# Attention and expert layer on one core: weights and x converted earlier, inside the attention units

## The chip, the cores and the metric

One core of one Trainium2 chip. The metric is the device time of one execution in microseconds. The time before is the median of three runs.

## The reference, cut to what matters

The kernel computes a multi-head attention with a position bias made by a small network, and feeds its result to an expert layer with a clipped quadratic activation. Shapes: batch 4, heads 8, sequence 576, head size 64; tokens 2304, model 512, hidden 2048; all float32.

```python
scores = scale * q @ k.T + bias            # bias from log distances, per head
attn = exp(scores - max) / (sum + 1e-9)
x = (attn @ v).transpose(0, 2, 1, 3).reshape(B * S, H * D)
h = x @ w_in
g = where(h >= 1, h, where(h <= -1, 0, (h + 1) ** 2 / 4))
out = g @ w_out
```

## The kernel before, in words

There are three stages. The first makes the bias in HBM. The second (lines 393 to 656) is attention: 16 units n, one for each pair of heads p = n // 4 and batch b = n % 4. A unit has five parts k of 128 query rows; each part is cut into two half-steps, `step(2 * k)` after its scores and `step(2 * k + 1)` after the queued transposes and value products have been drained. The text counts half-steps through as T = 10 n + i. TensorE makes scores (lines 431, 432, 452, 453), transposes of the exponentials (line 497) and value products (line 535); VectorE adds the bias and takes the maximum (line 434); ACT takes exponentials (line 441) and evicts; GpSimd subtracts to get the low halves (lines 131, 482). Every operand is kept as a high and a low part (fp32r), and three products make one.

The third stage is the expert layer (lines 661 to 751). It takes three blocks of 768 tokens, in each 16 blocks f of 128 hidden columns, and for each f two halves j of 384 tokens: `up_proj` (12 matmuls of 384 columns, lines 678 to 680), the activation (lines 687 to 691), `down_proj` (9 matmuls of 512 columns, lines 699 to 701). One such (f, j) is called a half-step of the expert stage; there are 96. It needs two things in SBUF. The weights of f: `weights(f)` calls `weight` for w_in and for w_out (lines 104 to 122): a load of 128 x 512 int64 (512 KB), two ACT operations that make floats of the two words (lines 113, 114), a VectorE join (line 115), an ACT cast to the high part (line 117), a GpSimd subtraction for the low part (line 118). And x of head pair k and half j: `split_x` (line 344) loads both heads' value products and the inverse sums that attention stored in HBM (`xT`, `rT`), adds, multiplies, casts to the high part on ACT (line 383) and subtracts for the low part.

The tables `XA` and `WT` of CFG say when this is done for the first two weight blocks and the first token block. Before the change that is in units 14 and 15: each x has a pair (unit, part) at which it is asked for and one at which it is made, and the weights of f = 0 and 1 are traced at unit 15, parts 1 and 4. Six of the eight x (mode 'p') are made with GpSimd doing add, multiply and subtraction (lines 378, 379, 385), pinned there by `pool` up to unit 14; the two of mode 'v' use VectorE (lines 381, 382, 387).

The order of instructions on an engine is set by the framework's scheduler, which takes what it believes ready, in the order written; `tc.keep_in_program_order` pins an instruction behind the one written before it on its engine. SP issues almost all DMAs, in order. One buffer each of the tags `raw`, `a` and `x` in the pool `rps[0]` serves both kinds of conversion; two bias tiles also use `x` (line 404). From the third block on, the weights are converted during the expert stage, in tiles that lie in memory which the attention stage holds (lines 662 to 670).

Of the kernel before, what the change touches and what calls it, by code (L numbers as in the profile page):

```python
# [30 lines left out]
CB = sum(CBW)  # L31
CFG = dict(un=('paaa',) * NG, xa=((((14, 0), (14, 1), '', 'p'), ((14, 2), (14, 4), '', 'p'), ((14, 4), (15, 0), '', 'p'), ((14, 3), (15, 1), 'bias', 'p')), (((15, 0), (15, 1), 'kh', 'p'), ((15, 0), (15, 2), 'kl', 'v'), ((15, 1), (15, 3), 'vs', 'p'), ((15, 1), (15, 4), '', 'v'))), ex=(9, 2, 0, 2, 9), bb=5, mv=1, hi='pvvpv', rb='a', lag=(1, 1), dr=(3, 1, 2, 2, 2), pool=((0, 1), (2, 0), (2, 1), (3, 0), (3, 1)), sb=4, keep=1, drain=2, diag='a', rb2='v', eps='v', rc=2, rbb=1, hb=2, rawb=(2, 2), t=(3, 10, 11, 10, 18, 11, 12, 19), eb=4, seq=0, pb=(6, 9, 12, 14, 16), pq=22, tb=6, ub=12, low0='ppp', anch=(8, 8, 16, 23, 23), low1='ppp', ob=6, gb=3, fin=2, wt=((15, 1), (15, 4)), lastp=15, xs=2, sbf=('v', 'v', 'v', 'v', 'v'), bsE=(), ytail='p')
EPS = 1e-9
RB = 2
LASTP = CFG["lastp"]
XA = CFG["xa"]
NX = [((14, 0), (14, 1), (14, 1), (15, 0)), ((4, 0), (6, 0), (8, 0), (10, 0))]
WT = CFG["wt"]
# [8 lines left out]
def attn_cpb_moe_kernel(ctx, tc, qk, vL, cb, win, wout, lw, ident, ii, out):  # L47
# [52 lines left out]
    def x_pool():  # L100
        turn[1] += 1
        return ring[turn[1] % len(ring)]

    def weight(src, dst, name):
# [12 lines left out]
        nc.scalar.copy(h, t.bitcast(F32))  # L117
        nc.gpsimd.tensor_tensor(out=l, in0=t.bitcast(F32), in1=h.bitcast(F32), op=ALU.subtract)  # L118

    def weights(f):  # L120
        weight(win[f], [x.rearrange("p a b -> p (a b)") for x in wi[f]], f"i{f}")
        weight(wout[f * P : f * P + P], wo[f], f"o{f}")
# [4 lines left out]
    def low(o, i, h, x="p"):  # L127
        if x == "v":
            nc.vector.tensor_tensor(out=o, in0=i, in1=h.bitcast(F32), op=ALU.subtract)
            return  # L130
        pool(nc.gpsimd.tensor_tensor(out=o, in0=i, in1=h.bitcast(F32), op=ALU.subtract))

    def pool(ins):
        if KEEP and go[0]:
            tc.keep_in_program_order(ins)
# [208 lines left out]
    def split_x(blk, k, j, early=False, raw=None):  # L344

        src = xT[k][blk // TB][:, :, TH * j : TH * j + TH].rearrange("(s d) i c -> d s i c", s=2)
        if raw is None:
            rp, n_ = x_pool()
            if n_:
                r = rp.tile([P, 3, TH], F32, tag="x", name=f"x{blk}_{k}_{j}", bufs=n_)  # L350
                r, rr = r[:, 0:2], r[:, 2]
            else:
                r = rp.tile([P, 2 * DM], F32, tag="raw", name=f"x{blk}_{k}_{j}")[:, : 2 * TH].rearrange("p (a b) -> p a b", a=2)
                rr = rp.tile([P, DM], F32, tag="a", name=f"xr{blk}_{k}_{j}")[:, :TH]
        else:
            r, rr = raw[:, 0:2], raw[:, 2]
# [12 lines left out]

        z = (2 * (blk // TB) + j) % 3  # L370
        h = x_tile(z, k, 0, f"xh{blk}_{k}_{j}")
        l = x_tile(z, k, 1, f"xl{blk}_{k}_{j}")
        xs[blk, k, j] = h, l
        x = r[:, 0]

        def parts():
            if early == "p":
                pool(nc.gpsimd.tensor_tensor(out=x, in0=x, in1=r[:, 1], op=ALU.add))
                pool(nc.gpsimd.tensor_tensor(out=x, in0=x, in1=rr, op=ALU.mult))
            else:  # L380
                nc.vector.tensor_tensor(out=x, in0=x, in1=r[:, 1], op=ALU.add)  # L381
                nc.vector.tensor_tensor(out=x, in0=x, in1=rr, op=ALU.mult)
            nc.scalar.copy(h, x)
            if early == "p":
# [4 lines left out]
        if early:  # L389
            return parts  # L390
        parts()

    with ExitStack() as ph:
        tp1 = ph.enter_context(tc.tile_pool(name="a_eT1", bufs=1))
# [131 lines left out]
        def values(n, half, es, eT, vs):  # L526
            hi, lo = eT
            b, p = n % B, n // B
            w = 256 + D * half
            x = sp.tile([P, 2, 320], F32, tag="x", name=f"x{n}_{half}", bufs=2)  # L530
            for j in range(2):
                ps = psO.tile([P, 512], F32, tag="T", name=f"O{n}_{half}_{j}")
                for src, first, last in ((hi, True, False), (lo, False, True)):
                    for tb in range(4):
                        nc.tensor.matmul(ps[:, :w], vs[:, 4 * j + tb, :], src[:, 4 * j + tb, :], start=first and tb == 0, stop=False)

                    nc.tensor.matmul(ps[:, :w], vs[:, 8 + j, :], src[:, 8, :], start=False, stop=last)
                nc.scalar.copy(x[:, j, :w], ps[:, :w])
            c0 = b * S + 256 * half
            c1 = c0  # L540
            while c1 < c0 + w:
                e = min(c0 + w, c1 - c1 % TB + TB)
                dst = xT[p][c1 // TB][:, :, c1 % TB : c1 % TB + e - c1]
                stores.append([CFG["xs"], dst, x[:, :, c1 - c0 : e - c0]])
# [6 lines left out]
        xe = {}  # L551

        def drain(keep, mid=None, at=0):
            while len(queue) > keep:
# [4 lines left out]
                    f()  # L559

        stores = []

        def store_x(all_=False):
            for s_ in stores:
                s_[0] -= 1
            while stores and (all_ or stores[0][0] < 0):
                _, dst, x = stores.pop(0)
                nc.sync.dma_start(out=dst, in_=x)

        def step(i_):  # L570
            store_x()
            for m in range(3):
                for t, i in STEPS:
                    if t == 20 - 10 * m + i_ and 0 < n + m < N:
                        preps[n + m][i]()

        go[0] = True
        for n in range(N):
# [6 lines left out]
            for k in range(5):  # L585
# [46 lines left out]
                    x[0] -= 1  # L632
                drain(CFG["dr"][k], exp_, CFG["ex"][k])
                exp_()
                last_e = exps[-1]
                step(2 * k + 1)
                for i in range(NK):
                    for j in range(2):
                        ask, make, home, e = XA[j][i]
                        if (n, k) == ask:  # L640
                            r = None
                            if home:
                                po, w, n_ = dict(kh=(qp, QW, CFG["hb"]), kl=(qp, QW, 2), vs=(qp, 10 * P, 2), bias=(bp, 2 * S, CFG["bb"]))[home]
                                r = po.tile([P, w], F32, tag=home, name=f"rx{j}_{i}", bufs=n_)
                                r = r[:, : 3 * TH].rearrange("p (a b) -> p a b", a=3)
                            xe[i, j] = split_x(0, i, j, e, r)
# [172 lines left out]
```

## Time and profile before

| | us |
|---|---|
| three runs | 770.16, 762.58, 764.74 |
| median | 764.74 |
| the profiled execution | 770.81 |
| its span | 769.0 |
| TensorE busy in the span | 717.0 |

The profile is of one execution, and its rows are times of that one. Busy time of TensorE counts instructions that overlap, so a stretch can be full and still leave small holes.

### The profile page before, as it was taken

What the parts mean: (1) busy time and instruction counts of PE and PEld (TensorE: products, weight loads), DVE (VectorE), ACT (ScalarE), POOL (GpSimd) and SP (SyncE); (2) the same over time, 40 slices, a digit from 0 to 9 for tenths busy, and PEclk for the clock granted to TensorE, in tenths of its full rate; (3) what the DMA queues carried; (4) which work ended last, traced back from release to release, by engine and by line L of the source; (5) the groups of instructions that cost most, each with busy time, mean ns of one, the idle gap of its engine ahead of it and who ended that gap; (6) DMA issues with size and microseconds to landing.
All of it is one profiled execution on the core that took longest, in us unless ns stands there. A gap on an engine that the chain in (4) does not pass through costs nothing. (4 is left out here: it accounts for less than half of the span.)

```text
span 769.0 us, 13382 instructions
## 1 busy us (share of the span) xinstructions
PE 717.0 (93%) x4688; PEld 635.8 (83%) x4688; DVE 445.7 (58%) x907; ACT 475.1 (62%) x1041; POOL 419.6 (55%) x362
## 2 busy tenths in 40 slices
PE   5677899899999999787899999999999999999997
PEld 2324899899999999775888889999998999989996
DVE  6998788778878888574665734663222243222222
ACT  7996889879989899596798562432222243222222
POOL 8985688858887888864688442222222222222221
PEclk9999999999999999898999999999999999999999
DMA  8887878956987887437665422461000011000002
GB/s 241 264 250 234 228 186 216 259 152 154 277 233 184 230 188 180 117 100 236 203 218 168 147 94 82 117 180 43 1 1 0 1 40 64 0 1 1 1 0 83
DMA packets 58515, 103.35 MB, mean 134 GB/s; under 512 B 12480, under 2 KB 32464, under 8 KB 58448
## 3 DMA queue, kind: packets, MB, share of 16 engines
q1 hardware_dynamic: 56000, 92.44, 41.7%
q0 software_dynamic: 2304, 9.96, 6.4%
q8 instruction: 37, 0.61, 0.4%
q14 instruction: 30, 0.25, 0.1%
q10 hardware_dynamic: 144, 0.09, 0.1%
HBM read 67.38 MB, written 25.12 MB: 120 GB/s over the span
## 5 line engine op out<-in xcount | busy, mean ns | idle before, releaser
L691 POOL TENSOR_TENSOR gl<-c,gh 128x384 fp32r<-128x384 f32 x96 | 100.7, 1049 | 243.1 <-ACT gh L690 222.3
L688 ACT ACTIVATE c<-c,half_s 128x384 f32<-128x384 f32 x96 | 59.0, 615 | 158.0 <-DVE c L687 157.4
L687 DVE TENSOR_SCALAR c<-h 128x384 f32<-128x384 f32 x96 | 53.2, 554 | 140.0 <-PE h L680 132.6
L482 POOL TENSOR_TENSOR lo<-c,hi 128x512 fp32r<-128x512 f32 x75 | 103.0, 1387 | 44.4 <-DVE hi L481 42.0
L678 PE MATMUL h<-xh,wi 128*128 128x384 f32 x352 | 120.1, 341 | 7.1 <-DVE c L689 4.3
L680 PE MATMUL h<-xh,wi 128*128 128x384 f32 x352 | 118.8, 338 | 0.5 <-POOL wi L118 0.5
L679 PE MATMUL h<-xl,wi 128*128 128x384 f32 x352 | 118.4, 336 | 0.3 <-DVE xl L387 0.3
L699 PE MATMUL y<-wo,gh 128*128 128x512 f32 x288 | 112.7, 393 | 2.6 <-ACT wo L117 2.6
L701 PE MATMUL y<-wo,gl 128*128 128x512 f32 x288 | 114.8, 399 | 0.0
L700 PE MATMUL y<-wo,gh 128*128 128x512 f32 x288 | 114.7, 398 | 0.0
L434 DVE CUSTOM_DVE_ANT_0 e<-S,bias 128x576 f32<-128x576 f32 x128 | 94.8, 751 | 23.6 <-PE S L432 22.2
L441 ACT ACTIVATE e<-e,mx 128x576 f32<-128x576 f32 x128 | 100.5, 787 | 11.5 <-DVE mx L434 11.3
L431 PE MATMUL S<-kh,qa 128*128 128x288 f32 x256 | 79.0, 327 | 7.8 <-DMA kh<-kh 4.2
L689 DVE TENSOR_TENSOR c<-h,c 128x384 f32<-128x384 f32 x96 | 53.3, 556 | 54.9 <-ACT c L688 54.7
L690 ACT CAST gh<-c 128x384 fp32r<-128x384 f32 x96 | 49.1, 512 | 52.6 <-DVE c L689 51.7
L678 PEld LDWEIGHTS h<-xh,wi 128*128 128x128 f32 x352 | 66.1, 188 | 15.8 <-DVE c L689 8.9
L432 PE MATMUL S<-ls,qa 128*128 128x288 f32 x256 | 74.4, 308 | 0.0
L497 PE MATMUL T<-id_s,e 128*128 128x128 f32 x512 | 69.3, 277 | 3.7 <-ACT e L441 3.7
L679 PEld LDWEIGHTS h<-xl,wi 128*128 128x128 f32 x352 | 66.1, 188 | 2.9 <-DVE xl L387 0.5
L680 PEld LDWEIGHTS h<-xh,wi 128*128 128x128 f32 x352 | 66.0, 188 | 0.9 <-POOL wi L118 0.8
L699 PEld LDWEIGHTS y<-wo,gh 128*128 128x128 f32 x288 | 54.6, 190 | 11.7 <-ACT wo L117 2.9
L701 PEld LDWEIGHTS y<-wo,gl 128*128 128x128 f32 x288 | 54.6, 190 | 11.6
(121 smaller groups left out, 1521.7 us busy)
## 6 DMA issues: line engine op xcount, KB each, us to landing
bias_d<-y SPq DMA_DIRECT2D x36, 295.5 KB, 4.6
qk<-in_qk_dram SPq DMA_DIRECT2D x16, 608.0 KB, 4.9
qa<-in_qk_dram POOLq DMA_DIRECT2D x16, 608.0 KB, 7.1
rawi<-in_win_dram SPq DMA_DIRECT2D x16, 512.0 KB, 4.1
rawo<-in_wout_dram SPq DMA_DIRECT2D x16, 512.0 KB, 3.8
x<-xT SPq DMA_DIRECT2D x40, 192.0 KB, 3.5
v<-in_vL_dram SPq DMA_DIRECT2D x16, 320.0 KB, 3.9
qa<-ls SPq DMA_DIRECT2D x32, 152.0 KB, 4.8
```

The source lines that it names most:

```text
L431: nc.tensor.matmul(ps[:, hf, :HS], qs[:, qc], kh[:, kc : kc + HS], start=True, stop=False)
L432: nc.tensor.matmul(ps[:, hf, :HS], q0[:, qc], kl[:, kc : kc + HS], start=False, stop=True)
L434: nc.vector.tensor_tensor_reduce(out=ev.rearrange("p (a b) -> p a b", a=2), in0=ps[:, :, :HS], in1=bias[k][:, S * j : S * j + S].rearrange ...
L441: lambda ev=ev, j=j: nc.scalar.activation(ev, ev, AF.Exp, bias=mx[:, j : j + 1], scale=-1.0, accum_out=sm[:, 4 * j + k : 4 * j + k + 1])
L482: r = nc.gpsimd.tensor_tensor(out=lo, in0=m, in1=hi.bitcast(F32), op=ALU.subtract)
L678: nc.tensor.matmul(ps[:, :TH], wh_, xh, start=k == 0, stop=False)
L679: nc.tensor.matmul(ps[:, :TH], wh_, xl, start=False, stop=False)
L680: nc.tensor.matmul(ps[:, :TH], wl_, xh, start=False, stop=k == NK - 1)
L691: nc.gpsimd.tensor_tensor(out=gl, in0=c, in1=gh.bitcast(F32), op=ALU.subtract)
L699: nc.tensor.matmul(y, gh[:, c], wo[f][0], start=f == 0, stop=False)
L700: nc.tensor.matmul(y, gh[:, c], wo[f][1], start=False, stop=False)
L701: nc.tensor.matmul(y, gl[:, c], wo[f][0], start=False, stop=f == NF - 1)
```

## The change

`XA` and `WT` go. Two tables of half-steps take their place: `XQ` for x (load at T, buffer, first operation at T1) and `WQ` for the weights (load at T, first operation at T1). `step` runs the jobs of its half-step. A weight piece has three: at T1 the two ACT operations, at T1 + 1 the join and the cast to the high part, both on VectorE (the cast was ACT's), at T1 + 2 GpSimd's subtraction. An x has three: add and multiply on VectorE, cast on ACT, subtraction on GpSimd, in consecutive half-steps. `keep` pins all of them except GpSimd's, which `pool` pins in units before the last; the loads are not pinned. The eight x use the buffers `raw`, `x` and one bias tile, and no longer those of k and v. Weight pieces: units 5, 6, 9 and 10. x: pairs 0, 1 and 2 of the first half in units 4, 8 and 12, the others in units 13, 14 and 15.

```diff
+XQ = {(0, 0): (39, "raw", 43), (1, 0): (79, "raw", 83), (2, 0): (118, "raw", 123), (3, 0): (137, "bias", 142),
+      (0, 1): (125, "x", 136), (1, 1): (131, "raw", 145), (2, 1): (139, "x", 151), (3, 1): (148, "raw", 155)}
+WQ = {(0, 0): (49, 53), (0, 1): (59, 63), (1, 0): (89, 93), (1, 1): (99, 103)}
...
+    def weight_ahead(f, o):
...
+        def load():
+            w["raw"] = rps[0].tile([P, DM, 2], I32, tag="raw", name=f"raw{f}{o}")
+            nc.sync.dma_start(out=w["raw"].rearrange("p a b -> p (a b)"), in_=src.bitcast(I32))
+
+        def shift():
+            raw = w["raw"]
+            w["a"] = rps[0].tile([P, DM], F32, tag="a", name=f"a{f}{o}")
+            keep(nc.scalar.activation(raw[:, :, 0], ...
+            keep(nc.scalar.activation(w["a"], ...
+
+        def join():
+            t = w["a"].bitcast(I32)
+            keep(nc.vector.scalar_tensor_tensor(out=t, in0=t, scalar=3, in1=w["raw"][:, :, 0], op0=ALU.logical_shift_left, op1=ALU.bitwise_or))
+            keep(nc.vector.tensor_copy(h, w["a"]))
+
+        def rest():
+            pool(nc.gpsimd.tensor_tensor(out=l, in0=w["a"], in1=h.bitcast(F32), op=ALU.subtract))
...
+        def scaled():
+            for op, in1 in ((ALU.add, r[:, 1]), (ALU.mult, rr)):
+                a = nc.vector.tensor_tensor(out=x, in0=x, in1=in1, op=op)
+                if home:
+                    keep(a)
+
+        def high():
...
+            a = nc.scalar.copy(xs[blk, k, j][0], x)
+            if home:
+                keep(a)
+
+        def rest():
+            h, l = xs[blk, k, j]
+            if home:
                 pool(nc.gpsimd.tensor_tensor(out=l, in0=x, in1=h.bitcast(F32), op=ALU.subtract))
...
+        for kj in XQ:
+            plan_x(*kj)
+        for fo, (T, T1) in WQ.items():
+            load, fs = weight_ahead(*fo)
+            plan(T, load)
+            for i, f in enumerate(fs):
+                plan(T1 + i, f)
...
         def step(i_):
             store_x()
+            for f in jobs.pop(10 * n + i_, ()):
+                f()
...
-                        if (n, k) == ask:
...
-                        if (n, k) == make:
-                            xe[i, j]()
-                for f in range(2):
-                    if (n, k) == WT[f]:
-                        with tc.issue_after(last_e.ins):
-                            weights(f)
```

## Rows read from the trace of the kernel before

**Rows 1.** Windows, one unit each: stretch, then length and busy us by engine, PEclk, DMA.

```profile
237.57:253.52 15.95, 15.86 (x126) 15.34 (x125) 13.41 (x34) 14.61 (x39) 13.38 (x12) 1.00 0.74 177
...
301.34:324.31 22.97, 18.98 (x126) 18.11 (x125) 15.06 (x33) 14.68 (x40) 20.00 (x19) 0.85 0.52 134
324.31:344.90 20.59, 16.85 (x127) 15.56 (x126) 14.23 (x33) 17.60 (x46) 13.38 (x14) 1.00 0.37 100
```

**Rows 2.** Timeline of unit 14 (ACT, GpSimd, VectorE): start, us, engine, line, [idle before].

```profile
310.61 0.51 ACT L383 CAST xh<-rx 128x384 fp32r<-128x384 f32 x1 [2.80 <-POOL rx L379]
...
314.71 0.51 ACT L383 CAST xh<-x 128x384 fp32r<-128x384 f32 x1 [3.11 <-POOL x L379]
...
325.56 0.51 ACT L383 CAST xh<-x 128x384 fp32r<-128x384 f32 x1 [2.05 <-POOL x L379]
...
306.71 2.92 POOL L131 TENSOR_TENSOR ls<-qk,kh 128x608 fp32r<-128x608 f32 x2
...
308.09 3.39 DVE L161 CAST vs<-v 128x640 fp32r<-128x640 f32 x1 [1.07 <-PE O L537]
```

**Rows 3.** Windows, the hand-over between the stages.

```profile
350.00:370.00 20.00, 13.91 (x55) 10.82 (x53) 9.18 (x15) 13.50 (x25) 7.21 (x6) 0.83 0.80 248
```

**Rows 4.** Waits of TensorE from 352 to 376: us in total, times, longest.

```profile
PE y L699 <- ACT wo L117: 2.6, 1, 2.6
PE h L678 <- DVE c L689: 2.0, 1, 2.0
PE h L678 <- ACT xh L383: 1.9, 1, 1.9
```

**Rows 5.** Chain that ended last, expert stage: start, us, what.

```profile
453.48 0.17 PE h L680
...
694.20 0.24 PE y L700
...
731.88 0.24 PE y L700
764.75 0.24 PE y L701
```

**Rows 6.** Timeline, end of the attention stage (TensorE, SP).

```profile
349.57 0.27 PE L521 MATMUL R<-id_s,sum 128*9 128x128 f32 x1
...
353.42 3.12 SPq L108 DMA_DIRECT2D rawi<-in_win_dram  x2
```

**Rows 7.** Timeline, single instructions of ACT, GpSimd and VectorE.

```profile
282.63 0.83 DVE L149 CAST kh<-qk 128x1216 fp32r<-128x1216 f32 x1
...
357.39 1.28 POOL L118 TENSOR_TENSOR wo<-ao,wo 128x512 fp32r<-128x512 f32 x1 [3.68 <-ACT wo L117]
...
357.85 0.77 ACT L113 ACTIVATE rawi<-rawi,floor_s 128x512 int32<-128x512 uint16 x1
358.52 0.66 ACT L114 ACTIVATE ai<-rawi 128x512 f32<-128x512 f32 x1
...
362.10 0.60 ACT L117 CAST wi<-ai 128x512 fp32r<-128x512 f32 x1
```

**Rows 8.** Instructions by source line: ns min/median/max, first to last start.

```profile
L115 DVE SCALAR_TENSOR_TENSOR ao<-ao,rawo x16: 678/693/912, 355.5 to 458.2; 128x512 int32<-128x512 int32 x16
...
L161 DVE CAST vs<-v x16: 484/1073/3394, 33.7 to 308.1; 128x640 fp32r<-128x640 f32 x16
...
L381 DVE TENSOR_TENSOR x<-x x17: 543/552/1646, 350.6 to 622.6; 128x384 f32<-128x384 f32 x17
...
L385 POOL TENSOR_TENSOR xl<-x,xh x3: 993/998/1012, 315.6 to 334.1; 128x384 fp32r<-128x384 f32 x3
...
L108 SPq DMA_DIRECT2D rawi<-in_win_dram x16: 327/328/1040, 4.5 to 408.3; - x16
```

**Rows 9.** Windows, four us within unit 4.

```profile
144.00:148.00 4.00, 3.92 (x30) 3.51 (x29) 4.00 (x11) 3.76 (x9) 2.01 (x2) 1.00 1.05 256
```

**Rows 10.** Timeline of TensorE at the end of unit 4.

```profile
152.58 0.38 PE L431 MATMUL S<-kh,qa 128*128 128x288 f32 x1 [2.13 <-DMA kh<-kh]
```

More of the change, by code (lines that the diff above doesn't have):

```diff
@@ L31 @@
 CB = sum(CBW)
-CFG = dict(un=('paaa',) * NG, xa=((((14, 0), (14, 1), '', 'p'), ((14, 2), (14, 4), '', 'p'), ((14, 4), (15, 0), '', 'p'), ((14, 3), (15, 1), 'bias', 'p')), (((15, 0), (15, 1), 'kh', 'p'), ((15, 0), (15, 2), 'kl', 'v'), ((15, 1), (15, 3), 'vs', 'p'), ((15, 1), (15, 4), '', 'v'))), ex=(9, 2, 0, 2, 9), bb=5, mv=1, hi='pvvpv', rb='a', lag=(1, 1), dr=(3, 1, 2, 2, 2), pool=((0, 1), (2, 0), (2, 1), (3, 0), (3, 1)), sb=4, keep=1, drain=2, diag='a', rb2='v', eps='v', rc=2, rbb=1, hb=2, rawb=(2, 2), t=(3, 10, 11, 10, 18, 11, 12, 19), eb=4, seq=0, pb=(6, 9, 12, 14, 16), pq=22, tb=6, ub=12, low0='ppp', anch=(8, 8, 16, 23, 23), low1='ppp', ob=6, gb=3, fin=2, wt=((15, 1), (15, 4)), lastp=15, xs=2, sbf=('v', 'v', 'v', 'v', 'v'), bsE=(), ytail='p')
+CFG = dict(un=('paaa',) * NG, ex=(9, 2, 0, 2, 9), bb=5, mv=1, hi='pvvpv', rb='a', lag=(1, 1), dr=(3, 1, 2, 2, 2), pool=((0, 1), (2, 0), (2, 1), (3, 0), (3, 1)), sb=4, keep=1, drain=2, diag='a', rb2='v', eps='v', rc=2, rbb=1, hb=2, rawb=(2, 2), t=(3, 10, 11, 10, 18, 11, 12, 19), eb=4, seq=0, pb=(6, 9, 12, 14, 16), pq=22, tb=6, ub=12, low0='ppp', anch=(8, 8, 16, 23, 23), low1='ppp', ob=6, gb=3, fin=2, lastp=15, xs=2, sbf=('v', 'v', 'v', 'v', 'v'), bsE=(), ytail='p')
 EPS = 1e-9
@@ L118, in weight @@
         nc.gpsimd.tensor_tensor(out=l, in0=t.bitcast(F32), in1=h.bitcast(F32), op=ALU.subtract)
+    def weight_ahead(f, o):
+        w = {}
+        src = wout[f * P : f * P + P] if o else win[f]
+        h, l = wo[f] if o else [x.rearrange("p a b -> p (a b)") for x in wi[f]]
+        def load():
[4 more added lines that the diff above has]
+            w["a"] = rps[0].tile([P, DM], F32, tag="a", name=f"a{f}{o}")
+            keep(nc.scalar.activation(raw[:, :, 0], raw.bitcast(U16).rearrange("p a (b c) -> p a b c", c=2)[:, :, 0, 1], AF.Identity, scale=2.0**-13, bias=floor_s))
+            keep(nc.scalar.activation(w["a"], raw[:, :, 1].bitcast(F32), AF.Prelu, scale=2.0**-112, alpha=-(2.0**32)))
+        def join():
[4 more added lines that the diff above has]
+            pool(nc.gpsimd.tensor_tensor(out=l, in0=w["a"], in1=h.bitcast(F32), op=ALU.subtract))
+        return load, (shift, join, rest)
     def weights(f):
@@ L131, in low, with keep @@
         pool(nc.gpsimd.tensor_tensor(out=o, in0=i, in1=h.bitcast(F32), op=ALU.subtract))
+    def keep(ins):
+        tc.keep_in_program_order(ins)
     def pool(ins):
@@ L342, in x_tile, with split_x @@
         return room[g][:, c0 : c0 + TH]
-    def split_x(blk, k, j, early=False, raw=None):
+    def split_x(blk, k, j, home=None):
         src = xT[k][blk // TB][:, :, TH * j : TH * j + TH].rearrange("(s d) i c -> d s i c", s=2)
-        if raw is None:
-            rp, n_ = x_pool()
-            if n_:
+        rp, n_ = x_pool() if home is None else (rps[0], home != "raw")
+        if n_:
+            if home == "bias":
+                r = bp.tile([P, 2 * S], F32, tag="bias", name=f"x{blk}_{k}_{j}").rearrange("p (a b) -> p a b", a=3)
+            else:
                 r = rp.tile([P, 3, TH], F32, tag="x", name=f"x{blk}_{k}_{j}", bufs=n_)
[L351 to L354, printed above, removed]
-        else:
-            r, rr = raw[:, 0:2], raw[:, 2]
+            r, rr = r[:, 0:2], r[:, 2]
+        else:
+            r = rp.tile([P, 2 * DM], F32, tag="raw", name=f"x{blk}_{k}_{j}")[:, : 2 * TH].rearrange("p (a b) -> p a b", a=2)
+            rr = rp.tile([P, DM], F32, tag="a", name=f"xr{blk}_{k}_{j}")[:, :TH]
         for i in range(2):
@@ L368, in split_x @@
             c1 = e
[L370 to L373, printed above, removed]
         x = r[:, 0]
[L376 to L384, printed above, removed]
+        def scaled():
[4 more added lines that the diff above has]
+        def high():
+            z = (2 * (blk // TB) + j) % 3
+            xs[blk, k, j] = [x_tile(z, k, i, f"x{'hl'[i]}{blk}_{k}_{j}") for i in range(2)]
+            a = nc.scalar.copy(xs[blk, k, j][0], x)
[4 more added lines that the diff above has]
+            if home:
                 pool(nc.gpsimd.tensor_tensor(out=l, in0=x, in1=h.bitcast(F32), op=ALU.subtract))
@@ L387, in parts @@
                 nc.vector.tensor_tensor(out=l, in0=x, in1=h.bitcast(F32), op=ALU.subtract)
-        if early:
-            return parts
-        parts()
+        if home:
+            return scaled, high, rest
+        scaled()
+        high()
+        rest()
     with ExitStack() as ph:
@@ L543, in values @@
                 dst = xT[p][c1 // TB][:, :, c1 % TB : c1 % TB + e - c1]
-                stores.append([CFG["xs"], dst, x[:, :, c1 - c0 : e - c0]])
+                stores.append([CFG["xs"], dst, x[:, :, c1 - c0 : e - c0], [(p, t) for t in range(c1, e)]])
                 c1 = e
@@ L550, in attn_cpb_moe_kernel @@
         queue, late = [], []
-        xe = {}
         def drain(keep, mid=None, at=0):
@@ L561, in attn_cpb_moe_kernel, with plan, plan_x, load @@
         stores = []
+        jobs = {}
+        made = set()
+        def plan(T, f):
+            jobs.setdefault(T, []).append(f)
+        def plan_x(k, j):
+            T, home, T1 = XQ[k, j]
+            def load():
+                assert all((k, t) in made for t in range(TH * j, TH * j + TH))
+                for i, f in enumerate(split_x(0, k, j, home)):
+                    plan(T1 + i, f)
[4 more added lines that the diff above has]
+            load, fs = weight_ahead(*fo)
+            plan(T, load)
+            for i, f in enumerate(fs):
+                plan(T1 + i, f)
         def store_x(all_=False):
@@ L566, in store_x @@
             while stores and (all_ or stores[0][0] < 0):
-                _, dst, x = stores.pop(0)
+                _, dst, x, of = stores.pop(0)
                 nc.sync.dma_start(out=dst, in_=x)
+                made.update(of)
         def step(i_):
             store_x()
+            for f in jobs.pop(10 * n + i_, ()):
+                f()
             for m in range(3):
@@ L634, in attn_cpb_moe_kernel @@
                 exp_()
-                last_e = exps[-1]
                 step(2 * k + 1)
-                for i in range(NK):
-                    for j in range(2):
-                        ask, make, home, e = XA[j][i]
-                        if (n, k) == ask:
[L641 to L646, printed above, removed]
-                        if (n, k) == make:
-                            xe[i, j]()
-                for f in range(2):
-                    if (n, k) == WT[f]:
-                        with tc.issue_after(last_e.ins):
-                            weights(f)
         queue += [x for _, x in late]
```

2 lines of the change are left out of this document (removed).

## The prediction

> **What bounds the kernel now.** I read the windows view first, one stretch per head pair and batch (a unit, cut at the reciprocal of its row sums). The reader sees [rows 1]: a quiet unit is 15.95 us long and TensorE is busy for 15.86 of them, so TensorE's own stream sets it; ACT leaves 1.34 us idle (14.61 busy), VectorE 2.54, GpSimd 2.57. Unit 14 takes 22.97 and unit 15 takes 20.59: 7.0 and 4.6 us over a quiet unit. In unit 14 GpSimd is busy for 20.00 and the granted clock is down to 0.85; in unit 15 ACT is the engine with the extra load (17.60).
>
> The timeline of unit 14 says why [rows 2]. ACT's cast of x (line 383) stands in its stream ahead of exponentials and waits for GpSimd's multiply three times: 2.80, 3.11 and 2.05 us, together 7.96, more than the whole excess. GpSimd is late because the pinned x work queues behind its 2.92 us of ls, and VectorE's cast of v takes 3.39 us beside it.
>
> Then the hand-over to the expert stage: the windows and the waits of TensorE [rows 3, 4]. From 350 to 370 us TensorE is busy for 13.91 of 20 at a granted clock of 0.83. It waits 2.6 us for the cast of the first w_out block, 2.0 for an activation, 1.9 for an x.
>
> Last the chain [rows 5]. In the expert stage nine half-steps take 731.88 - 694.20 = 37.68, so 4.187 each and 96 x 4.187 = 401.9 us in all; an up-projection matmul is 0.17. TensorE's last attention instruction stands at 349.57 [rows 6]; eleven of the stage's matmuls, 1.9 us, run before it. The last matmul ends at 764.75 + 0.24 = 764.99. So 764.99 - 349.57 = 415.4 us are spent on 400.0 us of work: 15.4 us are lost after the attention stage, 4 us of tail come on top, and the span of 769.0 lies inside 770.81 us.
>
> **The change, part by part.**
>
> *Taken out of units 14 and 15:* two weight blocks (four pieces of 128x512) and four of the eight x; GpSimd loses add and multiply of six x. One piece of weight costs ACT 0.77 + 0.66 + 0.60, VectorE 0.69 to 0.91, GpSimd 1.28; one x cost GpSimd or VectorE an add and a multiply, ACT 0.51, and a subtraction of 0.99 [rows 2, 7, 8].
>
> *Unit 14.* It now gets two x (pairs 3 and 1), each VectorE 2 x 0.55, ACT 0.51, GpSimd 0.99 [rows 2, 8]. Sums on a quiet unit [rows 1]: VectorE 13.4 + 2.2 = 15.6, GpSimd 13.4 + 2.0 = 15.4, ACT 14.6 + 1.0 = 15.6, all just under 15.95. No ACT cast stands behind GpSimd any more: the add and multiply are VectorE's and lie a half-step, 15.95 / 10 = 1.6 us, ahead. With three engines that full I don't expect the quiet time; bounds 15.95 and 22.97, taken at 17.5: gain 5.5.
>
> *Unit 15.* Two x remain; 0.77 + 0.66 + 0.60 = 2.0 us of weight conversion on ACT and two of four casts of x go. ACT falls from 17.60 to about 17.6 - 2.0 - 1.0 = 14.6 [rows 1, 2, 7]. Bounds 15.95 and 20.59; I take 16.7, near the quiet row: gain 3.9.
>
> *Hand-over.* Both blocks of weights and all eight x stand ready when TensorE ends attention, so the waits on wo and xh have nothing left to wait for, and where TensorE has no such waits the rows show a granted clock of 1.00 [rows 1], not 0.83. What is late next is the third weight block, whose tiles lie in memory that the attention stage holds to its end. Its raw load starts 353.42 - 349.57 = 3.85 us after that end [rows 6], its first conversion follows at 357.85, and 0.77 + 0.66 + 0.69 + 0.60 + 1.28 later it is ready [rows 7, 8]: 12.3 us after the end. The first four half-steps give TensorE 4 x 4.187 - 1.9 = 14.9 us of work until then. So it is covered by 2.6 us, if activations keep up. Of the 15.4 us lost I take 10 as won; bounds 4 (only the waits on wo and xh, 4.5, go) and 13.5 (the third block still costs something).
>
> *Weights in units 5, 6, 9 and 10.* Each such unit gets ACT 0.77 + 0.66 = 1.43 against 1.34 idle, VectorE 0.69 for the join and a cast that now is VectorE's (the nearest row is its cast of v, 0.48 to 3.39, median 1.07), GpSimd 1.28 [rows 1, 7, 8]. The idle time is in small pieces and each insertion delays exponentials or evictions that TensorE soon needs. Bounds 0 (work added to a unit that TensorE sets can't shorten it; the same holds for x) and 1.43 per unit; I take 0.8, over the middle because ACT becomes as full as TensorE: 3.2 in all, at most 5.7.
>
> *x in units 4, 8, 12 and 13.* Each adds 1.1 us on VectorE, 0.51 on ACT, 0.99 on GpSimd. Bounds 0 (inside 2.5 us of idle) and 1.6 (add, multiply and cast all on the path); I take 0.6: 2.4 in all, at most 6.4.
>
> *Loads.* Only the arithmetic is pinned. SP's loads are not: in the kernel before, the first w_in block, written in unit 15, was issued at 4.5 us, its first start [rows 8]. So a load goes out as soon as its buffer is free: the first weights right after the first x in unit 4, not in unit 5. There the DMA engines have a share of 1.05, and TensorE later waited 2.13 us for kh [rows 9, 10]. On SP, kh copies and the load of the next unit's qk are queued behind such a load. 512 KB more there cost between -1 (the load at 4.5 us is gone from the start) and 3 us; I take 0.5, since the copies of kh are written ahead of the load.
>
> A rule on VectorE and GpSimd speaks against the change. The row first: beside GpSimd's 2.92 us of ls, VectorE's cast of v took 3.39, where its shortest is 0.48 [rows 2, 8]. The Trainium skill, "SBUF — State Buffer", section "Who interferes with whom", says that a VectorE instruction with two SBUF inputs, or a cast in a two-port mode, and a GpSimd instruction that reads SBUF exclude each other for their whole length. All 24 VectorE instructions that the change places in the units (an add and a multiply for each of eight x, a join and a cast for each of four pieces) are of these kinds, and the trace agrees as far as that one row goes. By it they would run in turns with GpSimd, which is the second case below.
>
> *Sum:* gains 5.5 + 3.9 + 10 = 19.4; costs 3.2 + 2.4 + 0.5 = 6.1; net 13.3. The profiled execution's 770.81 becomes 757.5. It lies 6.1 us above the median of the three runs, so on 764.74 the same difference gives 751.4. One per cent of this, 7.6 us, is about what a measurement can tell from no change.
>
> **The rivals.**
>
> *VectorE and GpSimd take turns.* Then a unit lasts as long as both engines' exclusive work: GpSimd 13.4 plus VectorE's casts of kh and v, 0.83 + 1.07 = 1.9, is 15.3 today [rows 1, 7, 8]. A weight piece adds 1.28 + 0.69 + 0.6, so 17.9 (+1.9, four times 7.6); an x adds 0.99 + 1.1, so 17.4 (+1.4, four times 5.7); unit 14 with two x comes to 19.5 (gain 3.5, not 5.5). Net 3.5 + 3.9 + 10 - 7.6 - 5.7 - 0.5 = 3.6 gained: 761. For it: the 3.39 us cast. Against it: a late GpSimd delays only lo tiles that are used much later, so the sum need not reach TensorE.
>
> *The third weight block takes over the hand-over's idle time.* Activations and evictions of the last unit slow the first half-steps, the up-projection of the third block comes too early for its weights, and only 4 us are won there: 764.74 - 7.3 = 757.4. For it: 2.6 us of cover is little. Against it: TensorE has two down-projections in hand.
>
> *A pinned VectorE instruction waits for its x.* It stands at the head of an in-order engine; the score evictions, then exponentials and matmuls queue behind it. The loads of units 14 and 15 can only start when the last store of x has landed, and in units 4 and 8 they share DMA engines that are full. Unit 14 shows the price of such waits, 7.0 us. If it falls due in units 4, 8, 14 and 15, these last two win nothing and the first two lose 14: 14 + 6.1 - 10 = 10 us slower, 775. It decides as soon as a load lands more than a half-step, 1.6 us, after its make. Against it: four to seven half-steps, 6 to 11 us, lie between load and make.
>
> **How the numbers follow.** Forecast 0.68 (751.4; own range 744 to 757), turns 0.16 (761), third block 0.08 (757.4), late x 0.08 (775). Faster by over 1% means under 757.1: the forecast and half of the third-block case, 0.72. Within 1%: turns and the other half, 0.20. Slower: 0.08. The range, 742 to 762, leaves out the late x and the outer ends of the forecast (all gains at their upper bound less 1 us of costs would be 741).
>
> **What would show it.** Right: no ACT wait of over 1 us in unit 14, units 14 and 15 under 18 us, no TensorE wait on wo or xh after attention, granted clock near 1.00 there, the end of attention 3 us earlier and the loss after it about 5 us. Wrong: VectorE waiting on a DMA of x, weight units above 17.5 us, or new TensorE waits on the third block's wi.

## The result, and the profile after

| us | before | after |
|---|---|---|
| median of 20 runs each | 766.95 | 759.87 |
| lowest and highest | 762.58, 770.43 | 756.94, 764.44 |
| the profiled execution | 770.81 | 759.95 |
| its span | 769.0 | 758.2 |

The ratio is 0.9911, with a 95% interval of 0.9892 to 0.993: 7.1 us faster, where 13.3 were forecast. That is inside the range given, but only just within the 1% that stood for "no change".

The profile was read in three places that answer to the rows of before. First the hand-over. The windows view of the changed kernel (columns as in [rows 1]) gives the 20 us from just behind the end of attention, and the last two units' worth of time, cut at the reciprocals as there:

```profile
308.87:330.84 21.97, 19.30 (x146) 17.83 (x145) 19.59 (x43) 18.83 (x50) 19.95 (x17) 1.00 0.61 149
330.84:345.56 14.72, 14.05 (x97) 13.70 (x98) 11.12 (x26) 12.10 (x32) 2.47 (x3) 0.88 0.35 98
...
350.60:370.60 20.00, 18.85 (x100) 17.35 (x99) 11.87 (x19) 18.84 (x36) 15.67 (x12) 1.00 0.58 198
```

The last line answers to [rows 3]: TensorE is busy for 18.85 us instead of 13.91, at a granted clock of 1.00 instead of 0.83. The view of TensorE's waits from 352 to 376 us, whose three longest lines before are [rows 4], has one left:

```profile
PE h L721 <- DVE c L732: 1.2, 1, 1.2
```

The first two lines of the windows answer to the last two of [rows 1]: 36.69 us for the pair, where before it was 43.56.

Second, the units that received work. This is unit 5, then TensorE's waits from 140 to 308 us (us in total, times, longest), both of the changed kernel:

```profile
160.89:178.48 17.59, 16.44 (x126) 15.52 (x124) 16.01 (x35) 15.53 (x40) 14.26 (x13) 1.00 0.76 201
```

```profile
PE S L466 <- DVE mx L469: 3.5, 3, 1.6
PE S_L L487 <- DVE mx L469: 2.3, 2, 1.2
PE T L532 <- DVE lo L508: 0.8, 2, 0.4
```

A quiet unit is 15.95 us [rows 1]; this one is 17.59, and all its engines have over a microsecond idle. TensorE waits for score maxima (mx) from VectorE: 5.8 us in all, once each in units 4, 5, 8, 9 and 12, where the same view of the kernel before shows 0.5.

Third, lengths of the units, here cut where TensorE begins to transpose a unit's row sums (R; the first line of [rows 6] is the last of them). They are worked out from the timelines; "second profile" is the changed kernel, profiled again.

| us | before | after | second profile | x alone | weights alone |
|---|---|---|---|---|---|
| units 5, 6, 9, 10 (a weight piece each) | 63.94 | 69.81 | 69.36 | 63.79 | 68.84 |
| units 8, 12, 13 (x) | 48.08 | 51.91 | 52.30 | 51.33 | 55.09 |
| units 14 and 15 | 41.68 | 34.70 | 34.34 | 36.64 | 39.66 |
| last R to TensorE's end | 415.41 | 403.96 | 405.54 | 409.19 | 408.65 |

TensorE's end came 10.8 us earlier in the first pair of profiles (764.98 to 754.15). Of this 3.6 are unit 4's, 20.52 to 16.93. Before, that unit holds 2.6 us of waits for kh [rows 10] at a granted clock of 0.92. They belong to the execution: the kernel with the weights alone, below, is the kernel before up to the end of unit 4 and has 15.74 there, with no such wait. After, unit 4 holds an x, and that has a price which also differs by execution. Four kernels below that are alike up to unit 5 (x alone and the three with pure costs) have 16.71, 17.77, 19.03 and 17.79, and the longest wait of TensorE in each is one for a score maximum, 0.7 to 1.8 us. The other 7.2 of the 10.8 agree with the medians.

### The profile page after: what moved, and what is told of

It reads as the page before. It is cut to its first block, busy times and chain, and to the rows that moved or that the text cites. A ratio compares the mean times of both kernels' runs of the same rounds, so it can differ in the third digit from the quotient of the medians.

```text
span 758.2 us, 13397 instructions
## 1 busy us (share of the span) xinstructions
PE 712.8 (94%) x4688; PEld 631.5 (83%) x4688; DVE 457.0 (60%) x921; ACT 471.6 (62%) x1037; POOL 414.1 (55%) x352
## 4 chain that ended last, share of the span: by engine, by line
PE 63%; DMA 9%; DVE 6%; ACT 6%; issue 4%; POOL 3%; SPq 0%; DVEq 0%; ACTq 0%; POOLq 0%
PE y L743 7%; PE y L744 7%; PE y L742 7%; PE h L721 7%; PE h L723 7%; PE h L722 7%; PE O L570 7%; PE T L532 4%; PE S L466 3%; PE S L467 3%; DMA x<-xT 2%; DMA bias_d<-y 2%; DMA xT<-x 2%; PE O L572 2%; DMA rawo<-in_wout_dram 2%
## 5 line engine op out<-in xcount | busy, mean ns | idle before, releaser
L517 POOL TENSOR_TENSOR lo<-c,hi 128x512 fp32r<-128x512 f32 x75 | 101.2, 1365 | 33.9 <-DVE hi L516 31.4
L476 ACT ACTIVATE e<-e,mx 128x576 f32<-128x576 f32 x128 | 100.6, 790 | 11.7 <-DVE mx L469 11.5
L532 PE MATMUL T<-id_s,e 128*128 128x128 f32 x512 | 71.1, 275 | 2.0 <-DVE hi L516 1.0
L467 PE MATMUL S<-ls,qa 128*128 128x288 f32 x256 | 72.4, 301 | 0.0
L744 PEld LDWEIGHTS y<-wo,gl 128*128 128x128 f32 x288 | 54.0, 187 | 11.5
L532 PEld LDWEIGHTS T<-id_s,e 128*128 128x128 f32 x512 | 59.2, 142 | 4.6 <-DVE lo L508 1.3
```

The costliest lines, as they stand in the source:

```text
L467: nc.tensor.matmul(ps[:, hf, :HS], q0[:, qc], kl[:, kc : kc + HS], start=False, stop=True)
L476: lambda ev=ev, j=j: nc.scalar.activation(ev, ev, AF.Exp, bias=mx[:, j : j + 1], scale=-1.0, accum_out=sm[:, 4 * j + k : 4 * j + k + 1])
L517: r = nc.gpsimd.tensor_tensor(out=lo, in0=m, in1=hi.bitcast(F32), op=ALU.subtract)
L532: nc.tensor.transpose(ps[:, tb, :], e[:, c0 : c0 + P], id_s)
L744: nc.tensor.matmul(y, gl[:, c], wo[f][0], start=False, stop=f == NF - 1)
```

## The experiments

Each kernel ran beside the kernel before on one chip, where that took 768.76 to 769.60 us, so the ratios compare and the times do so only roughly.

**The two halves of the change.** Each kernel has one half and leaves the other as it was.

```diff
 x alone:
-        for fo, (T, T1) in WQ.items(): ...
+                for f in range(2):
+                    if (n, k) == ((15, 1), (15, 4))[f]: ... weights(f)
 weights alone:
-XQ = ...
+XA and the code that asks for x and makes it, as before
```

> Only x is made ahead; the two weight blocks are converted in unit 15 as before. Theory: units 5, 6, 9 and 10 fall back to 15.9 to 16.5 us (5.9 us less in all than with the weights in them), units 8, 12 and 13 keep 17.0 to 17.5, and the hand-over loses again the wait on the w_out block and what ACT does for it in unit 15, some 5 to 8 us: 759 to 763 us. Rival, that the hand-over is won by x alone: it stays short and the time is 753 to 756.

> Only the two weight blocks are converted ahead; x is made as in the kernel before. If the weights are paid for in their units (theory: each piece makes its unit about 1.4 us longer), units 5, 6, 9 and 10 last 17.1 to 18.0 us here too, unit 14 keeps its 25 us between two row-sum transposes, and only the wait on the w_out block and ACT's conversions leave the hand-over: 764 to 768 us. Rival, that the pieces cost nothing by themselves and the units are longer because of x: those four units are back at 15.9 to 16.5 us and the time is 759 to 762.

x alone: 760.31 us, ratio 0.9894 (0.9859 to 0.9929), as good as the whole change. Units 5, 6, 9 and 10 are quiet again: unit 5's window is 16.00 long,

```profile
156.80:172.80 16.00, 15.91 (x126) 15.40 (x124) 13.41 (x31) 14.59 (x38) 13.43 (x12) 1.00 0.82 210
```

So the weight pieces cost 69.81 - 63.79 = 6.0 us in those units, and return 5.2 after attention and 1.9 in units 14 and 15: about nothing on balance. Weights alone: 770.83 us, ratio 1.0033 (0.9999 to 1.0067), above what either theory had, even by the 769.24 us of the kernel before on this chip. Its unit 12 took 22.06. The timeline there (start, us, engine, what) says why:

```profile
277.30 0.53 SPq L108 DMA_DIRECT2D rawo<-in_wout_dram  x1
...
286.07 0.74 ACT L113 ACTIVATE rawo<-rawo,floor_s 128x512 int32<-128x512 uint16 x1 [4.59 <-DMA rawo<-in_wout_dram]
287.17 0.69 PE L540 MATMUL T_s<-id_s,e 128*128 128x128 f32 x2 [3.97 <-ACT x L567]
```

The next weight block, which nothing pins, was drawn forward from the expert stage into unit 12, where ACT waited 4.59 us for its load and TensorE 3.97 for ACT. In the changed kernel such a conversion first starts at 346.7. This kernel is therefore no clean measure of the weight half; with a quiet unit 12 it would lie at about 765, an estimate that takes this one profile's 6.1 us for every execution.

**The cast of the weights back on ACT.**

```diff
-            keep(nc.vector.tensor_copy(h, w["a"]))
+            keep(nc.scalar.copy(h, w["a"]))
```

> The cast of a weight piece goes back from VectorE to ACT, 0.60 us of ACT for 0.41 us of VectorE in each of units 5, 6, 9 and 10. Theory that VectorE and GpSimd in turns make these units long: ACT's 0.60 hides or nearly so, the four units change by -0.4 to +0.2 each and the time stays within 758 to 761. Rival that ACT is full and sets these units: each gets 0.6 longer, 762 to 763.

758.08 us, ratio 0.9852 (0.9799 to 0.9905). The four units sum to 66.88: 2.9 us less than in the changed kernel, more than the 1.6 that the theory allowed, with 0.60 us more on ACT in each. So ACT, the fullest engine by busy time, isn't what the pieces hurt.

**Pure costs in the quiet units.** Three kernels start from x alone and add two useless 128x512 instructions to each of units 5, 6, 9 and 10.

```diff
 two operands on VectorE:
+keep(nc.vector.tensor_tensor(out=t, in0=idb, in1=idb, op=ALU.add))
 one operand on VectorE:
+keep(nc.vector.tensor_reduce(out=scr[:, i : i + 1], in_=idb, op=ALU.max, ...))
 on ACT:
+keep(nc.scalar.copy(t, idb))
```

> Base: x made ahead, weights converted in unit 15, so that units 5, 6, 9 and 10 are quiet at 15.95 us. Added to each, in the half-step where the join of a weight piece stood: two VectorE instructions that read two SBUF operands of 128x512 and write one, about 0.6 us each when nothing is in their way. Nothing else of the weight piece is there. Theory that VectorE and GpSimd exclude each other: the two stand behind GpSimd's subtractions, show 0.6 to 1.6 us each, and the four units last 16.6 to 17.5. Rival that ACT's part or the load made the units of the weights long: they stay at 15.9 to 16.1.

> As the run with two-operand instructions, but the two VectorE instructions are reductions that read one SBUF operand of the same 512 elements. Theory that it is the second operand, and so GpSimd, that costs: they last about 0.6 us each wherever they stand, and the four units stay at 15.9 to 16.4, at most half of what the two-operand pair costs. Rival that any VectorE time in that place costs: the units are as long as with two operands.

> As the two runs before, but two ACT copies of 128x512, about 0.6 us each, take the place of the VectorE instructions: 1.2 us of ACT, near the 1.43 of a weight piece. Theory that ACT's idle 1.34 us take most of it: the four units last 15.95 to 16.4. Rival that ACT is full: 16.9 to 17.2.

One execution each (769.71, 761.91 and 766.34 us), so the unit lengths are what counts. On ACT, two copies of 0.61 us leave the four units at 15.85, 15.94, 15.95 and 15.94: nothing. The window of unit 5, and the added line by its source (ns, shortest, median, longest):

```profile
156.50:172.40 15.90, 15.81 (x126) 15.46 (x125) 13.38 (x32) 15.01 (x41) 12.65 (x11) 1.00 0.80 202
```

```profile
L621 ACT COPY probe<-id_s x8: 602/610/620, 165.0 to 246.7; 128x512 f32<-128x512 f32 x8
```

One-operand reductions on VectorE, 1.27 us a pair, make the units 16.56 to 17.12, 1.0 more on the mean: longer than the 16.4 that was expected, but under half of what two operands cost. Adds of two operands, in the same place, make three units 18.14 to 18.23, 2.2 more, and one 19.78, where the granted clock is 0.91 instead of 1.00. All lie above the expected 17.5. The timelines of the two kernels at that place (one operand first) show what differs:

```profile
159.79 1.30 POOL L517 TENSOR_TENSOR lo<-c,hi 128x512 fp32r<-128x512 f32 x1
...
159.84 1.27 DVE L621 TENSOR_REDUCE scr<-id_s 128x1 f32<-128x512 f32 x2
```

```profile
159.58 1.28 POOL L517 TENSOR_TENSOR lo<-c,hi 128x512 fp32r<-128x512 f32 x1
...
159.62 1.79 DVE L621 TENSOR_TENSOR probe<-id_s 128x512 f32<-128x512 f32 x1
...
161.94 0.67 DVE L621 TENSOR_TENSOR probe<-id_s 128x512 f32<-128x512 f32 x1
162.16 0.63 PE L532 MATMUL T<-id_s,e 128*128 128x128 f32 x4 [1.17 <-DVE lo L508]
```

Both meet a GpSimd subtraction at its start. The two reductions finish beside it, in 0.67 us each by source line. The first add takes 1.79, until 0.55 us after the subtraction's end (159.58 + 1.28 = 160.86, against 159.62 + 1.79 = 161.41); the second, with GpSimd idle, takes 0.67. All four pairs of adds show the same.

The add also writes 512 values a row where the reduction writes one, so this pair alone does not tell the second operand from the output. The trace of the adds does. VectorE's subtraction for the low half of a transpose has the add's shape and writes as much, but one of its operands, T, lies in PSUM:

```profile
L508 DVE TENSOR_TENSOR lo<-T,hi x53: 674/680/693, 76.6 to 345.3; 128x512 fp32r<-128x512 f32 x53
```

29 of the 53 start beside a GpSimd subtraction, and none is lengthened. Nor is every instruction with one operand free of GpSimd: the cast of v, from SBUF to SBUF, waits too. In the kernel before:

```profile
163.65 1.29 POOL L482 TENSOR_TENSOR lo<-c,hi 128x512 fp32r<-128x512 f32 x1
163.71 1.58 DVE L161 CAST vs<-v 128x640 fp32r<-128x640 f32 x1 [1.28 <-PE O L537]
```

Fourteen of its sixteen casts of v start beside a GpSimd subtraction and end 0.35 to 0.38 us after it, where the shortest cast takes 0.48 [rows 8].

**x on GpSimd, in the same half-steps.** Add and multiply of x go from VectorE to GpSimd.

```diff
-                a = nc.vector.tensor_tensor(out=x, in0=x, in1=in1, op=op)
+                a = (nc.gpsimd if home else nc.vector).tensor_tensor(out=x, in0=x, in1=in1, op=op)
                 if home:
-                    keep(a)
+                    pool(a)
```

> Add and multiply of the eight x go from VectorE to GpSimd, in the same half-steps. Theory that VectorE's two-input instructions pay for standing behind GpSimd's: units 8 and 12 lose their wait of TensorE for VectorE and shrink by 0.5 to 1.0 each, while unit 14, where GpSimd is fuller, gets 1 to 3 longer as ACT's cast waits for GpSimd again; 758 to 763. Rival that an x costs its unit the same wherever it is made: units 8 and 12 stay at 17.0 to 17.5 between two row-sum transposes.

764.96 us, ratio 0.9955 (0.9922 to 0.9988). Units 8 and 12 take 17.31 and 17.46, against 17.52 and 16.99: no shorter, as the rival had it, and unit 13 is 19.85. Unit 14 takes 22.79, 2.7 more than in the first profile of the changed kernel, as the theory had it. The timeline of ACT in unit 8:

```profile
215.74 0.51 ACT L411 CAST xh<-x 128x384 fp32r<-128x384 f32 x1 [1.91 <-POOL x L404]
```

This is the stall of [rows 2] again, now in the middle of attention: taking x off VectorE gives nothing where ACT then stands behind GpSimd.

**Later half-steps.** With the cast on ACT, three kernels move the weight pieces (`WQ`) and the x of units 4, 8 and 12 (`XQ`) within their units.

```diff
 both by three half-steps:   WQ first operation 53 -> 56, ...   XQ 43 -> 46, 83 -> 86, 123 -> 126
 weights by two:             WQ first operation 53 -> 55, ...   XQ as in the change
 weights by two, x by three: WQ first operation 53 -> 55, ...   XQ 43 -> 46, 83 -> 86, 123 -> 126
```

> The changed kernel with the cast of the weights on ACT, and with the weight pieces and the x of units 4, 8 and 12 made three half-steps later in their units, where GpSimd waits about 2 us for VectorE in a quiet unit. Theory of the turns: join, add and multiply show 0.55 to 0.8 us instead of 0.85 to 1.73, units 5, 6, 9 and 10 fall to 15.95 to 16.4 and units 8 and 12 to 16.0 to 16.5, so 2 to 4 us less than with the cast alone: ratio to the kernel before 0.978 to 0.984. Rival that the place within the unit makes no difference: units as with the cast alone, ratio 0.985.

> The kernel with the cast of the weights on ACT, with the weight pieces of units 5, 6, 9 and 10 begun at half-steps 55, 65, 95 and 105 (join at 56, 66, 96, 106) instead of 53, 63, 93 and 103. Theory (what a piece costs is VectorE's time, and the join runs long only when it meets a GpSimd instruction): at half-step 6 GpSimd has its idle time ahead of the low halves, so the join takes about 0.7 us instead of 0.9 to 1.4, and the four units sum to 65.5 us or less (quiet 63.8, cast on ACT 66.9); ratio to before 0.980 to 0.986. Rival (the join's length sets nothing, any inserted instruction costs about 0.7 us a unit by pushing the next score eviction back): the four units stay at 66.5 to 67.5, whatever the join takes; ratio 0.984 to 0.988.

> The kernel with the cast of the weights on ACT, weight pieces begun at half-steps 55, 65, 95 and 105, and x of units 4, 8 and 12 begun at 46, 86 and 126 instead of 43, 83 and 123. Theory (each VectorE microsecond put into a unit lengthens it by nearly as much, and its length is short where GpSimd idles): the four weight units sum to 66.0 to 66.6 (quiet 63.8), units 8 and 12 to 16.4 to 16.9 each as in the kernel with both later (17.3 and 17.4 with x at 83 and 123); the units of this kernel are then 3.5 + 1 us shorter than those of the changed kernel, ratio to the changed kernel on the same chip 0.991 to 0.997. Rival (what is won in the units is lost again after attention, where the kernel with both later took 405.7 instead of 404.0): same as the changed kernel, ratio to it 0.998 to 1.002.

> The changed kernel as it is, beside the kernel with the weight pieces at half-steps 55, 65, 95 and 105, for a comparison on one chip. Theory: 4 to 5 us slower than that kernel (its four weight units sum to 69.8 against 66.3, units 8 and 12 to 34.5 against 33.4), ratio to before 0.989 to 0.993. Rival: within 1.5 us of it. In either case the profile shows whether unit 4 (16.93 in the first profile of this kernel, 20.52 in that of the kernel before) is long in another execution too: if so, the wait for kh there belongs to the execution, not to the change.

Both by three: 755.87 us, ratio 0.9846 (0.9799 to 0.9893), above the 0.978 to 0.984 that was expected; the join now takes 1.41 us in every unit, since it meets a GpSimd subtraction each time, and the four units sum to 67.52. Weights by two: 757.54, ratio 0.9887 (0.9828 to 0.9945). There the join is short each time, as the theory wanted,

```profile
L139 DVE SCALAR_TENSOR_TENSOR a<-a,raw x4: 681/686/687, 160.7 to 246.2; 128x512 int32<-128x512 int32 x4
```

but the units sum to 66.30, not under 65.5: nearer to the rival. Weights by two and x by three: 759.08, ratio 0.9861 (0.9825 to 0.9897), with the changed kernel at 759.34 beside it on the same chip: no difference. Its join is as short (0.69), but the four units sum to 67.61, and TensorE's waits for kh are back there (4.5 us in all from 140 to 300). What was won in the units did not reach the total, as the rival had it; its time after attention was 406.09, the changed kernel's 405.54. The repeat of the changed kernel has unit 4 at 17.83, with a wait of 1.85 us for a score maximum and none over 0.3 for kh, and 69.36 for the four weight units.

**One x moved out of unit 14.**

```diff
-(1, 1): (131, "raw", 145), (2, 1): (139, "x", 151)
+(1, 1): (143, "bias", 150), (2, 1): (139, "x", 152)
```

> The kernel with the cast of the weights on ACT, with the x of pair 1, second half, made in unit 15 (half-steps 150 to 152) instead of unit 14 (145 to 147). That leaves one x in unit 14 and three in unit 15. Theory (what is left of unit 14's excess is the price of its two x pieces, about 2 us for each, among them TensorE's 1.6 us wait for a value product's operand and the lower granted clock behind it): unit 14 falls from 20.1 to 18 us or less, unit 15 rises by 1 to 2, TensorE's 1.6 us wait at the end of unit 14 is gone; total within 0.5% of the kernel with the cast on ACT (ratio to before 0.980 to 0.990). Rival (unit 14's excess is not from the x: it comes from the end of attention itself, where no further unit's loads and transposes fill TensorE's holes): unit 14 stays at 19.5 to 20.5, unit 15 gets longer by 1 to 2 us, ratio 0.987 to 0.992.

760.63 us, ratio 0.99 (0.9863 to 0.9938), unit 14 at 21.63. It tells nothing of the x pieces' price, for two reasons: by the cut used here half-steps 150 and 151 still lie in unit 14, and the loads of the moved x came late. Its timeline shows VectorE waiting, and TensorE behind it:

```profile
320.83 2.52 SPq L397 DMA_DIRECT2D xr<-rT  x4
321.57 0.56 DVE L404 TENSOR_TENSOR x<-x 128x384 f32<-128x384 f32 x1 [1.39 <-DMA x<-rT]
322.05 0.68 DVE L516 CAST hi<-T 128x512 fp32r<-128x512 f32 x1
...
322.88 1.09 PE L532 MATMUL T<-id_s,e 128*128 128x128 f32 x4 [2.11 <-DVE hi L516]
...
324.25 0.44 PE L466 MATMUL S<-kh,qa 128*128 128x288 f32 x1
```

A wait of 1.39 us at the head of VectorE became 2.11 on TensorE, and after it a score matmul takes 0.44 instead of 0.29: from 323 to 327 us the granted clock is 0.50, which is 1.2 GHz. So the rival "a pinned VectorE instruction waits for its x", which did not occur in the changed kernel's full units, has a real price when it does.

No version here is told apart from the change: those with the cast on ACT have ratios of 0.985 to 0.990, the changed kernel 0.9911 and 0.9878, and all these intervals overlap.

## Why the prediction was right or wrong

**Hand-over: right in size, and in its main reason.** The chain from the last R to the end went from 415.41 to 403.96 us, in the second profile to 405.54: 11.5 and 9.9 won, where 10 was taken. The waits on wo and xh are gone and the clock is at 1.00. What was said of the third weight block did not hold. The load at 353.42 [rows 6] that was taken for its own is, by the order in which the loads are written, that of the second block: only the first block's two loads, at 4.51 and 350.21, stand before it. In the changed kernel all w_in loads of line 109 belong to the third block or later ones. The first two go out 6 us before the end of attention at 350.19, so the tiles for the raw words did not wait for it, and the first low half of a w_in block is done at 355.95 + 1.30 = 357.25:

```profile
343.91 1.04 SPq L109 DMA_DIRECT2D rawi<-in_win_dram  x2
...
349.68 0.77 ACT L114 ACTIVATE rawi<-rawi,floor_s 128x512 int32<-128x512 uint16 x1 [1.13 <-DMA rawi<-in_win_dram]
...
355.95 1.30 POOL L119 TENSOR_TENSOR wi<-ai,wi 128x512 fp32r<-128x512 f32 x1
```

That is 7.1 us after the end, where 12.3 was reckoned, and TensorE waits for no wi. So the rival of the third block fell by a wider margin than the 2.6 us of cover, for a reason that the prediction did not have.

**Units 14 and 15: too high by a quarter.** 5.5 + 3.9 = 9.4 was taken; the pair gained 7.0 and 7.3 in the two profiles (6.9 by the cut of [rows 1]). Unit 15 went below the quiet time; unit 14 did not reach 17.5. No ACT cast waits 2 to 3 us for GpSimd there any more (one waits 1.00 for VectorE's multiply), but x's multiply runs long on VectorE. The timeline of the changed kernel:

```profile
328.49 2.83 POOL L517 TENSOR_TENSOR lo<-c,hi 128x512 fp32r<-128x512 f32 x2
...
328.54 1.65 DVE L404 TENSOR_TENSOR x<-x 128x384 f32<-128x384 f32 x1
...
331.07 1.16 PE L570 MATMUL O<-hi,vs 128*128 128x320 f32 x4 [1.59 <-DVE sum L677]
332.02 0.47 PE L572 MATMUL O<-hi,vs 128*128 128x320 f32 x1
...
335.47 0.31 PE L572 MATMUL O<-lo,vs 128*128 128x320 f32 x1
```

It takes 1.65 us beside GpSimd's subtractions, where 0.55 was counted; VectorE's low halves and the reciprocal of the sums queue behind it, TensorE waits 1.59 us, and then takes 0.47 instead of 0.31 for a matmul. The windows view shows why, a granted clock of 0.50, or 1.2 GHz:

```profile
332.00:334.00 2.00, 2.00 (x9) 2.00 (x9) 1.87 (x4) 0.87 (x3) 0.30 (x1) 0.50 0.11 17
```

That the long multiply causes the wait is read from this order, and no experiment shows it. Ten profiles have these x at these half-steps: in all of them the multiply takes 1.64 or 1.65 and the wait is 1.59 or 1.60. In two of them (two-operand adds, ACT copies) add and multiply of the unit's first x take 1.11 us together instead of 1.78 to 1.86, and their unit 14 is the shortest, 17.86 and 17.84 against 18.60 to 20.29.

**Weights in units 5, 6, 9 and 10: the step that failed.** 0.8 us each was taken, on the ground that "ACT becomes as full as TensorE", and the upper bound of 1.43 was ACT's time alone. Measured: 5.9 us for the four, 1.5 each, above that bound. ACT's time is free (1.21 us added, nothing lost); it is VectorE's that is on the path, though VectorE had 2.54 us idle. The mean over the four units:

| kernel | VectorE time added, us | unit longer than 15.95, us |
|---|---|---|
| ACT copies | 0 | -0.03 |
| weights by two half-steps, cast on ACT | 0.69 | 0.63 |
| weights by two, x by three, cast on ACT | 0.69 | 0.95 |
| the change, cast on ACT | 1.03 | 0.77 |
| one-operand reductions | 1.27 | 1.00 |
| both by three half-steps, cast on ACT | 1.41 | 0.93 |
| the change | 1.78 | 1.50 |
| two-operand adds (three units) | 2.46 | 2.22 |

In six of the seven kernels that give VectorE time the unit grows by 0.66 to 0.91 us for each microsecond of it. The seventh, 0.95 for 0.69, has the join of the row above it and a further wait: in each of the four units TensorE waits 0.37 us for a low half that GpSimd makes (us in total, times, longest):

```profile
PE O L570 <- POOL lo L517: 1.5, 4, 0.4
```

So GpSimd's part of a piece, 1.28 us, may cost something as well; no kernel adds it alone. The timeline of unit 5 in the changed kernel shows the path of VectorE's part:

```profile
162.09 0.74 DVE L469 CUSTOM_DVE_ANT_0 e<-S,bias 128x576 f32<-128x576 f32 x1
...
162.72 1.28 POOL L517 TENSOR_TENSOR lo<-c,hi 128x512 fp32r<-128x512 f32 x1
...
162.95 1.60 DVE L139 SCALAR_TENSOR_TENSOR a<-a,raw 128x512 int32<-128x512 int32 x1
...
164.47 0.74 DVE L469 CUSTOM_DVE_ANT_0 e<-S,bias 128x576 f32<-128x576 f32 x1
...
165.28 0.40 PE L487 MATMUL S_L<-kh,qa 128*128 128x288 f32 x1 [1.15 <-DVE mx L469]
```

The join meets GpSimd's subtraction and takes 1.60 us for its 0.69. The next score eviction stands behind it, and the next scores need the buffer that this eviction empties: TensorE waits 1.15, and as long in unit 9. In units 6 and 10 and in both kernels with VectorE instructions as pure costs the eviction that TensorE waits for is another, the low half that VectorE takes from a transpose (`lo`): 0.4 us in the change, 1.17 behind the two adds. VectorE's idle time in the quiet unit of [rows 1] is made of waits of its own, in the kernel before:

```profile
DVE vs L161 <- PE O L537: 1.1, 1, 1.1
DVE e L434 <- PE S L432: 0.9, 2, 0.6
DVE lo L473 <- POOL lo L482: 0.5, 1, 0.5
```

It lies where VectorE stands for TensorE and GpSimd; that time is no cover for work put in ahead of an eviction at another place.

**x in units 4, 8, 12 and 13: the same fault.** 0.6 each was taken; 3.8 and 4.2 us for the last three were measured, 1.3 to 1.4 each, and unit 4 lies 1.0 and 1.9 over a quiet unit. Moved by three half-steps, to a place where add and multiply take 0.55 us each, unit 12 is 16.45 and 16.48 in the two kernels that do so, where nine profiles with the early place have 16.99 to 17.50. Unit 8 is 16.86 and 18.35, inside the 16.79 to 18.99 of the early place, so nothing is settled there.

**The turns rival was nearest.** It gave 1.9 for a weight unit and 1.4 for one with an x, and 761 in all. Its mechanism stands, by the pure costs: VectorE work with two operands in SBUF waits for GpSimd, a reduction with one doesn't. The Trainium skill, "SBUF — State Buffer", section "Who interferes with whom", says that VectorE instructions with two SBUF inputs and GpSimd's SBUF reads exclude each other for their whole length; by that rule the add at 159.62 should end its own 0.67 after 160.86, at 161.53, and it ends at 161.41. What was argued against this rival was that a late GpSimd delays only low halves, needed much later. That looked at the wrong engine: it is VectorE that waits, and its evictions are needed at once. But taking turns is only part: even the pieces whose join met nothing cost 0.63 and 0.95 a unit.

**Loads: no cost seen, where 0.5 was taken.** The first weight load went out at 150.32, in unit 4, and no VectorE instruction in units 4 to 14 waited for an x; one in unit 15 waited 2.48 us, and TensorE did not wait there.

*The sum:* 11.5 + 7.0 won less 5.9 and 3.8 paid is 8.8 in the first pair of profiles; with the second profile of the changed kernel it is 9.9 + 7.3 - 5.4 - 4.2 = 7.6. The x of unit 4, 1.0 and 1.9, comes off: 7.8 and 5.7. The medians say 7.1. The forecast's gains were about right (19.4 against 18.5 and 17.2); its price for pieces in the units, 3.2 + 2.4 = 5.6, should have been 10.7 to 11.5. So the pieces cost the attention stage more than units 14 and 15 gave back. Its end, forecast 3 us earlier, came at 350.19 instead of 349.57, although the kernel before had lost 4.6 us to kh in unit 4, and the whole gain was made after it.

## What to carry to other kernels

The idle time of an engine in a full, balanced loop is cover only if it doesn't lie in front of something the bounding engine is about to need: ask which instruction stands next behind the inserted one, and price the insertion at its length there, on the engine that evicts, not by idle shares. Before moving work between engines, add the bare cost to a quiet stretch (two useless instructions a unit) and read the stretch's length; that told ACT (free) from VectorE (0.8 to 0.9 us per us) at once. A piece that is moved out of a stall saves the stall and pays its own price where it lands: here the weight pieces returned 7.1 us and paid 6.0 in one profile each, and the kernel without them is as fast (ratio 0.9894 against 0.9911).

## What the runs showed of the hardware

A VectorE instruction with two operands in SBUF that starts beside a GpSimd subtraction waits for it nearly to its end: 1.79 us against 0.67 for an add, 1.60 against 0.69 for a join, up to 1.73 against 0.55 for an add or multiply of x. With VectorE first it is GpSimd that waits: in the kernel with both by three half-steps, three multiplies of x that began 0.16 us ahead of a GpSimd subtraction of 128x512 kept their 0.55 us, and the subtraction took 1.54 or 1.55 instead of 1.28. A reduction with one operand in SBUF keeps its 0.67 us beside GpSimd, and so does a subtraction with one of its two operands in PSUM (0.67 to 0.69). A cast with one operand need not: the casts of v waited as the two-operand instructions did. A VectorE cast of a weight piece, 128x512 from SBUF to SBUF, bounded beforehand by 0.48 and 3.39 us, took 0.41 to 0.42 in all four places, none of which met a GpSimd instruction.

TensorE's granted clock fell to 0.50, or 1.2 GHz, behind a wait of 1.59 us in unit 14 of the changed kernel.
